# Issuing the 21 transfers that clear the output from GpSimd in one burst instead of from SP among the weights

## The chip, the cores and the metric

The kernel runs on one core of a Trainium2 chip. The metric is the device time of one execution in microseconds. The kernel before takes 942.89 us, the median of three runs (942.83 to 943.75). One more execution was taken with the hardware profiler; all rows below come from that one.

## What is computed

Two branches on the same 2048 x 512 input, mixed by a gate per token. Branch A is a short causal convolution of k, times v, then a long causal convolution per channel (an FFT in the reference) and a product with q. Branch B is a mixture of eight experts with two chosen per token, each a gated MLP with F = 1376 hidden columns.

```python
def _B_ref(x, w_router, w_gate, w_up, w_down):
    logits = jnp.einsum("bsd,de->bse", x, w_router)
    topk_idx = jnp.argsort(logits)[..., -2:]
    gates = _softmax(jnp.take_along_axis(logits, topk_idx, axis=-1), axis=-1)
    ...
    hg = _silu(jnp.einsum("bsd,edf->bsef", x, w_gate))
    hu = jnp.einsum("bsd,edf->bsef", x, w_up)
    y_all = jnp.einsum("bsef,efd->bsed", hg * hu, w_down)
    return jnp.einsum("bse,bsed->bsd", gate_dense, y_all)

x = A_q
g = _sigmoid((x * gate_w).sum(-1, keepdims=True))
a = _A_ref(x, A_k, A_v, A_shift_k, A_ssm_k, A_ssm_D)
b = _B_ref(x, B_w_router, B_w_gate, B_w_up, B_w_down)
return g * a + (1 - g) * b
```

## The kernel before

The eight experts run one after the other (variable `r`), each over eleven tiles of F of 128 columns (`ft`; the last has 96). For a tile, one transfer brings the gate and up weights (`raw`, 512 KB) and one the down weights (`rd`, 256 KB). ScalarE (ACT) rounds them to `gh` and `dh`, VectorE (DVE) computes the remainders `gl` and `dl`, and TensorE (PE) multiplies three times for each product: rows by `gh`, rows by `gl`, remainder of the rows by `gh`. The two products of a half of the rows are `g` and `u`; ACT and DVE make `sg`, `hh` and `hl` of them. After each group of three tiles the down products `yp` go through three PSUM buffers into the sums `ya`, by DVE from the second group on.

The tokens of an expert are fetched by GpSimd (POOL) with indirect transfers (`xg`, five for each expert, L511), turned by TensorE (`xgp`, L520) and split into `xh` and `xl`. The first expert is chosen and gathered ahead of all others, while the routing of the rest is still being worked out (`routing`, `places`, `read_lists`). Results are added into the output rows by indirect transfers from POOL (`add_rows`, L720), so the output, 2688 rows, has to be zero first: `clear` writes 21 blocks of 128 rows from `zt`, a tile of zeros. The first of the adding transfers stands at 168.8 us of the span.

Branch A fills the gaps: `fill` is a list of generators of which `tick` runs a step behind each F tile. `k_stage1` and `x_stage1` are its first stages; `x_stage1` loads the taps `sk` and rows `krow` and `v`, forms `tmp` and `acc` on DVE and splits them into `xs`. Results go through DRAM (`kd`, `xd`, `zd`) between stages. Nine writes left over from the first stages (`rest_k`: `kd` from `ks1`, `ks3`, `ks5`, `ks9`, `ks10` and the load `cr`) are issued by POOL behind the rounding of weight tiles 4, 5 and 6 of the first expert (`behind_rows` adds a wait on the instruction kept in `anchor`; `gh 0 6` is the rounding of tile 6).

SP issues the weights, `krow`, `v` and, in the kernel before, the clearing transfers, in one queue in order; POOL issues in its own. Every transfer of an issuing engine also carries one of eight semaphores in turn, so that it waits for the one that stands eight places earlier to have landed. Up to the end of `order` the instructions stand as written; behind it a scheduler with a model of times orders each engine's instructions, so moving a transfer changes what stands around it. Buffers limit how early SP may load: three for `raw`, two for `rd`; `sk` is also scratch for `places` and is loaded again only behind it.

Of the kernel before, what the change touches and what calls it, by code (L numbers as in the profile page):

```python
# [24 lines left out]
P = 128  # L25
# [12 lines left out]
ROWS = S + TILES * P  # L38
# [15 lines left out]
LG, LR = (2, 5)  # L54
BUB = (1, 1, 3)
XG = 3
Z0, Z1 = (7, 6)
RM = 5
K0, LATE = (4, 3)
SEQ_N = 10  # L60
# [78 lines left out]
def gated_mix(ctx: ExitStack, tc: tile.TileContext, a, out):  # L139
    nc = tc.nc  # L140
    sync, act, dve, pool, pe = nc.sync, nc.scalar, nc.vector, nc.gpsimd, nc.tensor
# [342 lines left out]
    def tick():  # L484
        if fill:
            live.append(fill.pop())
        for g in list(live):
            if next(g, live) is live:
                live.remove(g)
# [3 lines left out]
    def after(engine):  # L493
        return nullcontext() if ordered or engine not in anchor else tc.issue_after(anchor[engine])


    def behind_rows(i, name="act rest"):
        tc.add_manual_dep(i, anchor[name].name, mybir.DependencyInfo(
            mybir.DependencyClass.Sync, mybir.DependencyReason.DATA), reason="behind the gather")

    def tiles(r):
        return (CAPS[r] + P - 1) // P
# [31 lines left out]
    def gather(r):  # L534
        xh = wp.tile([P, KT, CM], F32R, tag="xh", bufs=2, name=f"xh{r}")
        xl = wp.tile([P, KT, CM], F32R, tag="xl", bufs=2, name=f"xl{r}")
        xs[r] = (xh, xl)
        g = [load_rows(r, n) for n in range(XG - 1 if r else tiles(0))]
        for n in range(tiles(r)):
            yield  # L540
            if len(g) < tiles(r):
                g.append(load_rows(r, len(g)))
            turn_rows(r, n, g[n], xh, xl)
# [347 lines left out]
    def places(g):  # L891
        if not g:
            table["hot"] = wp.tile([P, 2, LK, P], F32R, tag="xl", bufs=2, name="hot")
            table["val"] = wp.tile([P, LK, 3, NT], F32R, tag="xh", bufs=2, name="val")
            table["list"] = ps.tile([P, D], F32, tag="y", bufs=3, name="list")[:, :3 * NT]
        hot, val = table["hot"][:, g % 2], table["val"]
        hotc = sk.rearrange("p t d -> p (t d)")[:, g % 2 * 2 * D:][:, :LK * NT].rearrange("p (i c) -> p i c", i=LK)
        part = slice(g * LK, g * LK + LK)
        s3 = [P, LK, NT]
        with after("dve"):  # L900
            dve.tensor_tensor(hot, fl(row)[:, part].unsqueeze(2).to_broadcast([P, LK, P]),
                              io128.unsqueeze(1).to_broadcast([P, LK, P]), op=ALU.is_equal)
            dve.tensor_tensor(hotc, fl(colf)[:, part].unsqueeze(2).to_broadcast(s3),
                              cols.unsqueeze(1).to_broadcast(s3), op=ALU.is_equal)
        for f in range(3):
            dve.tensor_mul(val[:, :, f], hotc, fl(pay[:, f])[:, part].bitcast(F32).unsqueeze(2).to_broadcast(s3))
        for i in range(LK):
            pe.matmul(table["list"], hot[:, i], val[:, i].rearrange("p f c -> p (f c)"),
                      start=(g + i == 0), stop=(g * LK + i == n2 - 1))

    def read_lists():
        pv = table["list"].rearrange("p (f c) -> p f c", f=3)
        dve.tensor_scalar(idf, pv[:, 0], dummy, None, op0=ALU.add)
        dve.tensor_scalar(gidx[:, TILES:], idf[:, TILES:MAIN], float(S - 1), None, op0=ALU.min)
        dve.scalar_tensor_tensor(wsum, idf, float(S), spare, op0=ALU.is_ge, op1=ALU.mult)
        dve.tensor_add(sidx, idf, wsum)
        dve.tensor_copy(wsum, pv[:, 1])
        dve.tensor_add(slot_w, wsum, pv[:, 2])
# [17 lines left out]
    i = dve.tensor_scalar(gidx[:, :TILES], pv0, float(S), float(S - 1), op0=ALU.add, op1=ALU.min)  # L936
# [131 lines left out]

    lv = fp.tile([P, 2 * P], I32, tag="mi", bufs=3, name="lv")[:, :2 * OVER].rearrange("p (o c) -> p o c", c=2)
    def clear(i):  # L1070
        with after("sp"):
            sync.dma_start(out[i * P:(i + 1) * P, :], zt)

    mp = mp_ctx.enter_context(tc.tile_pool(name="moe", bufs=1))
    zt = mp.tile([P, D], F32, tag="yr", bufs=4, name="zt")
# [8 lines left out]
    for r in range(E):  # L1084
        x = expert(r) if r else first
        up, down, finish = x.up, x.down, x.finish
        if r:
            x.begin()
        ends = {g[-1]: i for i, g in enumerate(GROUPS[r])}
        for ft in range(len(FT)):  # L1090
            up(ft)
            for _ in range(min(2, len(tasks))):
                f, *args = tasks.pop(0)
                f(*args)
            if ft in ends:
                tasks.append((down, ends[ft]))
            if r + 1 < E:
                if r == 0:
                    for _ in range(CH.count(ft)):
                        with after("dve rest"), after("act rest"):  # L1100
                            next(rest, None)
                    if 0 <= ft - LG < n2 // LK:
                        places(ft - LG)
                    if ft == LR:
                        read_lists()
                if (r, ft) == (0, LR):
                    dve.tensor_copy(lv[:, :, 0], sidx[:, MAIN:])
                    dve.tensor_copy(lv[:, :, 1].bitcast(F32), slot_w[:, MAIN:])
                    sync.dma_start(lst, lv)
                if ft == (G0 if r == 0 else 4):  # L1110
                    ahead = gather(r + 1)
                if ft >= (G0 if r == 0 else 4):
                    next(ahead, None)
            if r == 0:
                for f in rest_k[LATE * (ft - K0):LATE * (ft - K0 + 1)] if ft >= K0 else ():
                    behind_rows(f.write().ins, f"gh 0 {ft}")
            seen += 1
            if r == 0 and ft >= Z0:
                for i in range(Z1 * (ft - Z0), min(Z1 * (ft - Z0 + 1), ROWS // P)):
                    clear(i)  # L1120
            while done < min(total, int(total * seen / n_up)):
                tick()
                done += 1
        if r not in TM:
            tasks += [(finish, n) for n in range(4)] + [(lambda: None,)] + [(finish, n) for n in range(4, tiles(r))]
# [96 lines left out]
```

## Time and profile before

| | |
|---|---|
| median of three runs | 942.89 us (942.83 to 943.75) |
| profiled execution | 943.57 us, of it 941.3 us span |
| PE busy | 923.5 us, 98% of the span |
| DVE busy | 633.6 us, 67% |
| ACT busy | 509.7 us, 54% |
| POOL busy | 146.6 us, 16% |
| the clearing transfers | 21 of 256 KB, issued by SP from 64.5 to 109.9 us |

Times in the rows are microseconds from the start of the span. A busy share of an engine over the whole span is an average over stages; what matters for a transfer at 64 to 110 us is which engine sets the pace there and at what time the data that this transfer delays is needed. Of an issuing engine the timeline shows when a transfer was issued, not when it landed.

### The profile page before, as it was taken

To read this page: it belongs to the slowest core of one execution; us is meant where nothing else is said; L and a number is where in the kernel's file an instruction comes from. 1 tells how busy PE (TensorE), PEld (TensorE's weight loads), DVE (VectorE), ACT (ScalarE), POOL (GpSimd) and SP (SyncE) were. 2 spreads that over 40 slices of the span, in tenths; PEclk is the share of its full clock that TensorE was granted. 3 is DMA by queue.
4 is the path that set the end of the run, shared out by engine and by line. 5 is a ranking of instruction groups with operands and counts; after the bars stand their busy time and mean duration, and the time that the engine had idled before them with its cause. 6 is when DMAs were issued, how large, how long until landed. Compare 5 with 4: busy or idle time off the path is not lost. (4 is left out here: it accounts for less than half of the span.)

```text
span 941.3 us, 18097 instructions
## 1 busy us (share of the span) xinstructions
PE 923.5 (98%) x6957; PEld 830.0 (88%) x6957; DVE 633.6 (67%) x1131; ACT 509.7 (54%) x883; POOL 146.6 (16%) x137
## 2 busy tenths in 40 slices
PE   8999999999999999999999999999999999999996
PEld 4679999999999999978898889888887989889984
DVE  4796699999996557556767666765777645554541
ACT  4654334755456546478656876668766544234330
POOL 0320210300003020131101211013010310121012
PEclk9999999999999999999999999999999999999999
DMA  9895945754456463456445655456553786787233
GB/s 329 301 349 220 376 153 191 207 193 155 140 202 183 157 205 122 135 135 204 144 136 169 166 181 175 141 167 174 182 172 121 188 276 181 193 200 217 70 54 45
DMA packets 76378, 172.02 MB, mean 183 GB/s; under 512 B 8481, under 2 KB 9377, under 8 KB 76162
## 3 DMA queue, kind: packets, MB, share of 16 engines
q1 hardware_dynamic: 53490, 121.89, 38.4%
q0 software_dynamic: 12464, 29.02, 13.6%
q10 hardware_dynamic: 10336, 19.93, 5.8%
q8 instruction: 56, 0.92, 0.4%
q14 instruction: 32, 0.26, 0.1%
HBM read 127.24 MB, written 43.57 MB: 181 GB/s over the span
## 5 line engine op out<-in xcount | busy, mean ns | idle before, releaser
L200 PE MATMUL u<-xh,gh 128*128 128x256 f32 (+14 forms) x704 | 202.0, 287 | 2.5 <-ACT sg L642 2.5
L200 PE MATMUL g<-xh,gh 128*128 128x256 f32 (+17 forms) x696 | 200.8, 288 | 1.9 <-DVE sg L643 1.9
L202 PE MATMUL u<-xh,gl 128*128 128x256 f32 (+14 forms) x704 | 201.3, 286 | 0.0
L201 PE MATMUL u<-xl,gh 128*128 128x256 f32 (+14 forms) x704 | 201.1, 286 | 0.0
L202 PE MATMUL g<-xh,gl 128*128 128x256 f32 (+17 forms) x696 | 198.8, 286 | 0.0
L201 PE MATMUL g<-xl,gh 128*128 128x256 f32 (+17 forms) x696 | 198.6, 285 | 0.0
L200 PEld LDWEIGHTS g<-xh,gh 128*128 128x128 f32 (+1 forms) x696 | 129.5, 186 | 8.8 <-DVE sg L643 4.5
L200 PEld LDWEIGHTS u<-xh,gh 128*128 128x128 f32 (+1 forms) x704 | 130.9, 186 | 5.9 <-ACT sg L642 3.1
L201 PEld LDWEIGHTS u<-xl,gh 128*128 128x128 f32 (+1 forms) x704 | 130.9, 186 | 4.3 <-issue 4.1
L202 PEld LDWEIGHTS g<-xh,gl 128*128 128x128 f32 (+1 forms) x696 | 129.6, 186 | 4.3 <-issue 4.1
L202 PEld LDWEIGHTS u<-xh,gl 128*128 128x128 f32 (+1 forms) x704 | 131.1, 186 | 0.9 <-issue 0.8
L201 PEld LDWEIGHTS g<-xl,gh 128*128 128x128 f32 (+1 forms) x696 | 129.5, 186 | 2.4 <-issue 0.8
L642 ACT ACTIVATE sg<-g 128x256 f32<-128x256 f32 (+14 forms) x176 | 68.0, 387 | 111.9 <-PE g L202 110.6
L200 PE MATMUL yp<-hh,dh 128*128 128x264 f32 (+13 forms) x440 | 127.1, 290 | 0.0
L202 PE MATMUL yp<-hh,dl 128*128 128x264 f32 (+13 forms) x440 | 126.8, 289 | 0.0
L201 PE MATMUL yp<-hl,dh 128*128 128x264 f32 (+13 forms) x440 | 126.8, 288 | 0.0
L644 ACT ACTIVATE hh<-sg 128x256 fp32r<-128x256 f32 (+14 forms) x176 | 73.1, 418 | 98.6 <-DVE sg L643 98.0
L643 DVE TENSOR_TENSOR sg<-sg,u 128x256 f32<-128x256 f32 (+14 forms) x176 | 74.8, 426 | 72.2 <-PE u L202 70.7
L584 ACT ACTIVATE gh<-raw 128x1024 fp32r<-128x1024 f32 (+1 forms) x88 | 91.4, 1038 | 50.8 <-PE u L201 50.0
L590 DVE TENSOR_TENSOR gl<-raw,gh 128x1024 fp32r<-128x1024 f32 (+1 forms) x88 | 105.3, 1197 | 18.6 <-ACT gh L584 17.8
L645 DVE TENSOR_TENSOR hl<-sg,hh 128x256 fp32r<-128x256 f32 (+14 forms) x176 | 75.0, 429 | 24.8 <-ACT hh L644 24.5
L653 DVE TENSOR_TENSOR dl<-rd,dh 128x512 fp32r<-128x512 f32 (+1 forms) x88 | 59.5, 685 | 39.8 <-ACT dh L651 39.7
(283 smaller groups left out, 1549.6 us busy)
## 6 DMA issues: line engine op xcount, KB each, us to landing
raw<-in_wgu SPq DMA_DIRECT2D x80, 512.0 KB, 4.4
rd<-in_wd SPq DMA_DIRECT2D x80, 256.0 KB, 4.3
kl<-kd SPq DMA_DIRECT2D x16, 512.0 KB, 5.2
xl<-xd SPq DMA_DIRECT2D x32, 256.0 KB, 4.1
zd<-ze ACTq DMA_DIRECT2D x16, 512.0 KB, 3.9
zl<-zd SPq DMA_DIRECT2D x16, 512.0 KB, 5.9
out<-zt SPq DMA_DIRECT2D x21, 256.0 KB, 6.1
krow<-in_kpad SPq DMA_DIRECT2D x19, 256.0 KB, 5.5
```

The costliest lines, as they stand in the source:

```text
L200: pe.matmul(p, wh, hi, start=start, stop=False)
L201: pe.matmul(p, wh, lo, start=False, stop=False)
L202: return pe.matmul(p, wl, hi, start=False, stop=stop)
L584: anchor[f"gh {r} {ft}"] = act.activation(st["gh", ft], raw, AF.Copy).ins
L590: dve.tensor_sub(st["gl", ft][:, c], raw[:, c], st["gh", ft][:, c].bitcast(F32))
L642: act.activation(sg[:fw, :nn], pp[0][:fw, :nn], AF.Silu)
L643: dve.tensor_mul(sg[:fw, :nn], sg[:fw, :nn], pp[1][:fw, :nn])
L644: act.activation(hh[:fw, sl], sg[:fw, :nn], AF.Copy)
L645: dve.tensor_sub(hl[:fw, sl], sg[:fw, :nn], hh[:fw, sl].bitcast(F32))
L653: dve.tensor_sub(dl[:fw], rd[:fw], dh[:fw].bitcast(F32))
```

## The change

`clear` no longer stands in SP's queue. All 21 clearing transfers are issued from POOL when the loop reaches tile 6 of the first expert, each with a wait on `gh 0 6`, behind the nine leftover writes. Before, SP issued six of them behind each of the tiles 7, 8, 9 and the last three behind tile 10 in the order of the source, which the scheduler spread over the queue.

```diff
-Z0, Z1 = (7, 6)
+Z0 = 6
...
     def clear(i):
-        with after("sp"):
-            sync.dma_start(out[i * P:(i + 1) * P, :], zt)
+        return pool.dma_start(out[i * P:(i + 1) * P, :], zt)
...
-            if r == 0 and ft >= Z0:
-                for i in range(Z1 * (ft - Z0), min(Z1 * (ft - Z0 + 1), ROWS // P)):
-                    clear(i)
+            if (r, ft) == (0, Z0):
+                for i in range(ROWS // P):
+                    behind_rows(clear(i).ins, f"gh 0 {Z0}")
```

POOL's queue, the difference from before (-) to after (+), with the gathers `xg` of the second expert (`xg_0` to `xg_4`) behind the last leftover writes:

```order
 L270 DMA kd<-ks10e 256x1x512
 L984 DMA cr<-in_c_r 128x256
+L1071 DMA out<-zt 128x512 x17
 L511 DMA xg_0_1197<-in_q,gidx 128x512
 L511 DMA xg_1_1199<-in_q,gidx 128x512
 L511 DMA xg_2_1380<-in_q,gidx 128x512
-L511 DMA xg_3_1474<-in_q,gidx 128x512
-L511 DMA xg_4_1571<-in_q,gidx 44x512
+L1071 DMA out<-zt 128x512 x4
+L511 DMA xg_3_1495<-in_q,gidx 128x512
+L511 DMA xg_4_1586<-in_q,gidx 44x512
```

Seventeen clearing transfers now stand ahead of the second expert's first gather and four ahead of its fourth.

SP's queue before, from the weights of tile 7 to the rows of the short convolution (`ISA` rows set registers):

```order
L573 DMA raw_8_1495<-in_wgu 128x1024
L623 ISA
L623 DMA rd_8_1565<-in_wd 128x512
L1072 DMA out<-zt 128x512 x6
L573 ISA
L573 DMA raw_9_1586<-in_wgu 128x1024
L1072 DMA out<-zt 128x512 x2
L623 ISA
L623 DMA rd_9_1656<-in_wd 128x512
L1072 DMA out<-zt 128x512 x4
L354 DMA sk<-in_sk 128x2048
L224 DMA krow_1770<-in_kpad 128x512
```

The same place in SP's queue after:

```order
L573 DMA raw_8_1510<-in_wgu 128x1024
L623 ISA
L623 DMA rd_8_1580<-in_wd 128x512
L573 ISA
L573 DMA raw_9_1595<-in_wgu 128x1024
L354 DMA sk<-in_sk 128x2048
L224 DMA krow_1773<-in_kpad 128x512
L623 ISA
L623 DMA rd_9_1665<-in_wd 128x512
L224 DMA krow_1775<-in_kpad 128x512
L224 DMA krow_1777<-in_kpad 128x512
L224 DMA krow_1779<-in_kpad 128x512
```

`sk` and the rows follow directly on the weights of tile 9, with no clearing transfers between.

On DVE the scheduler has answered by moving the short convolution (`tmp`, `acc`) of the first block up, between the additions `ya` of the second group of tiles; this is a piece of the difference:

```order
 L645 TENSOR_TENSOR hl_6_1223<-sg_6_1_1281,hh_6_1222 128x312
+L363 TENSOR_TENSOR tmp_1867<-krow_1777,sk 128x512
 L680 TENSOR_TENSOR ya_0_886<-yp_1_0_256_1303,ya_0_886 128x312
 L680 TENSOR_TENSOR ya_1_909<-yp_1_1_0_1314,ya_1_909 128x256
+L361 TENSOR_TENSOR acc_1866<-krow_1779,sk 128x512
 L680 TENSOR_TENSOR ya_1_909<-yp_1_1_256_1325,ya_1_909 128x312
+L364 TENSOR_TENSOR acc_1866<-acc_1866,tmp_1867 128x512
+L363 TENSOR_TENSOR tmp_1867<-krow_1775,sk 128x512
+L364 TENSOR_TENSOR acc_1866<-acc_1866,tmp_1867 128x512
 L680 TENSOR_TENSOR ya_2_932<-yp_1_2_0_1336,ya_2_932 128x256
```

Ten such operations stand ahead of the last addition of this group (`ya_3`, 312 columns) after, and two before.

On PE the turns `xgp_0` and `xgp_1` of the second expert's rows, of which the first stood within the product `g_7_1` of tile 7 and the second behind the last product of that tile, now stand together within the last product of tile 8, and `xgp_2` behind it:

```order
L200 MATMUL u_8_1_1562<-xh_433,gh_8_1512 128x312
L201 MATMUL u_8_1_1562<-xl_434,gh_8_1512 128x312
L202 MATMUL u_8_1_1562<-xh_433,gl_8_1514 128x312
L200 MATMUL u_8_1_1562<-xh_433,gh_8_1512 128x312
L520 MATMUL xgp_0_1382<-ident,xg_0_1197 128x128 x4
L520 MATMUL xgp_1_1497<-ident,xg_1_1199 128x128 x4
L201 MATMUL u_8_1_1562<-xl_434,gh_8_1512 128x312
```

Both turns now come four matmuls into `u_8_1`, one F tile later than before.

## Rows read from the trace of the kernel before

**Rows 1.** The page, busy time of each engine over the span, and the waits of PE over the whole span (engine, line, what it waited for: us in total, times, longest).

```profile
PE 923.5 (98%) x6957; PEld 830.0 (88%) x6957; DVE 633.6 (67%) x1131; ACT 509.7 (54%) x883; POOL 146.6 (16%) x137
...
PE u L200 <- ACT sg L642: 2.5, 3, 1.6
PE g L200 <- DVE sg L643: 1.9, 2, 1.2
PE xgp L520 <- DMA xg<-in_q,gidx: 1.2, 1, 1.2
```

**Rows 2.** Busy time by stretch: us of the stretch, then busy us (instructions) of PE, PEld, DVE, ACT, POOL, then granted clock, DMA share, GB/s.

```profile
60.00:70.00 10.00, 8.75 (x58) 6.98 (x54) 10.00 (x19) 4.56 (x7) 2.72 (x6) 1.00 0.97 356
...
64.00:320.00 256.00, 256.00 (x1949) 250.84 (x1948) 219.25 (x393) 131.17 (x241) 39.08 (x32) 1.00 0.62 204
320.00:840.00 520.00, 517.48 (x3965) 458.71 (x3965) 329.24 (x539) 314.45 (x510) 79.61 (x74) 1.00 0.55 171
```

**Rows 3.** Timeline of SP's queue (start, us, line, transfer, count).

```profile
64.45 4.98 SPq L1072 DMA_DIRECT2D out<-zt  x6
...
84.11 0.35 SPq L573 DMA_DIRECT2D raw<-in_wgu  x1
85.08 5.40 SPq L1072 DMA_DIRECT2D out<-zt  x6
90.72 1.10 SPq L573 DMA_DIRECT2D raw<-in_wgu  x1
...
98.90 1.62 SPq L354 DMA_DIRECT2D sk<-in_sk  x1
```

**Rows 4.** Timeline of POOL, with the idle time before and its releaser.

```profile
59.73 1.12 POOL L272 DMA_DIRECT2D kd<-ks1e  x2
...
85.81 0.68 POOL L270 DMA_DIRECT2D kd<-ks9e  x1 [15.54 <-ACT gh L584]
86.38 0.83 POOL L270 DMA_DIRECT2D kd<-ks10e  x1
86.94 0.84 POOL L984 DMA_DIRECT2D cr<-in_c_r  x1
94.99 1.04 POOL L511 DMA_INDIRECT xg<-in_q,gidx  x1 [7.21 <-PE g L202]
...
122.02 3.36 POOL L511 DMA_INDIRECT xg<-in_q,gidx  x1 [5.30 <-PE xgp L520]
```

**Rows 5.** Time from issue to landing: transfers issued from 84 to 96 us, one after the other (KB each, us), and the gathers issued from 60 to 130 us.

```profile
kd<-ks9e POOLq DMA_DIRECT2D x1, 512.0 KB, 6.9
kd<-ks10e POOLq DMA_DIRECT2D x1, 512.0 KB, 8.2
cr<-in_c_r POOLq DMA_DIRECT2D x1, 128.0 KB, 8.7
...
DMA to landing us min/median/max: 5.3/6.6/6.9
```

**Rows 6.** DMA queues, packets, MB and share of 16 engines: POOL's (q0) and SP's (q1) from 36 to 50 us, when both had work throughout. Then the same stretch and three later ones by engine, in the columns of Rows 2.

```profile
q0 software_dynamic: 720, 2.62, 47.8%
q1 hardware_dynamic: 914, 2.45, 46.6%
...
36.00:50.00 14.00, 14.00 (x98) 12.11 (x97) 10.46 (x38) 7.83 (x15) 3.62 (x5) 1.00 1.02 394
...
84.00:96.00 12.00, 12.00 (x98) 12.00 (x98) 8.97 (x22) 4.96 (x9) 2.99 (x4) 1.00 0.93 341
96.00:104.00 8.00, 8.00 (x61) 8.00 (x61) 4.04 (x8) 2.26 (x4) 1.97 (x3) 1.00 1.04 392
...
112.00:120.00 8.00, 8.00 (x60) 7.07 (x59) 8.00 (x15) 5.05 (x9) 2.02 (x2) 1.00 0.97 316
```

**Rows 7.** Timeline of PE: the first two turns of the second expert's rows and what follows each, a down product of the second group that takes a PSUM buffer again, and the first matmul of the second half of tile 8 (`g_8_1`).

```profile
105.03 0.29 PE L200 MATMUL yp<-hh,dh 128*128 128x256 f32 x1
...
112.31 0.60 PE L520 MATMUL xgp<-ident,xg 128*128 128x128 f32 x4
112.66 0.39 PE L200 MATMUL g<-xh,gh 128*128 128x312 f32 x1
...
114.90 0.60 PE L520 MATMUL xgp<-ident,xg 128*128 128x128 f32 x4
115.43 1.13 PE L293 MATMUL ks0p<-kr,c 64*128 64x512 f32 x4
...
119.41 0.31 PE L200 MATMUL g<-xh,gh 128*128 128x312 f32 x1
```

**Rows 8.** Timeline of DVE with idle time before, and its busy time from 101.5 to 110.5 us (us, busy us, instructions, clock, DMA share, GB/s).

```profile
87.49 1.22 DVE L590 TENSOR_TENSOR gl<-raw,gh 128x1024 fp32r<-128x1024 f32 x1
...
101.93 0.91 DVE L680 TENSOR_TENSOR ya<-yp,ya 128x312 f32<-128x312 f32 x2
...
110.57 0.69 DVE L363 TENSOR_TENSOR tmp<-krow,sk 128x512 f32<-128x512 f32 x1 [1.51 <-DMA krow<-in_kpad]
111.18 0.68 DVE L653 TENSOR_TENSOR dl<-rd,dh 128x512 fp32r<-128x512 f32 x1
111.78 0.69 DVE L361 TENSOR_TENSOR acc<-krow,sk 128x512 f32<-128x512 f32 x1
...
101.50:110.50 9.00, 3.14 (x8) 1.00 1.04 403
```

## The prediction

> **What bounds the kernel now.** I read the waits of PE and its busy time by stretch first, then the two queues that issue the clearing transfers, and last the places where PE or DVE first needs something that those transfers can delay.
>
> PE is busy for 98% of the span, and the stretch that matters is tighter than that: from 64 us, just before the first clearing transfer is issued, to 320 us PE is busy for all of its 256.00 us, and no wait of PE is listed there [rows 1, 2]. The reader should keep this apart from what SP does in the same stretch. SP issues its first six clearing transfers in 4.98 us and six more in 5.40 us, 0.8 to 0.9 us each where one weight transfer takes 0.35 us, and the weights of tile 9 follow at 90.72 us, although the last reader of their buffer (`gl` of tile 6, from 87.49 for 1.22 us) ended at 88.7 us [rows 3, 8]. So the clearing transfers do hold up SP by 2 us or so. But no one waits for what SP brings later: `sk`, issued at 98.90 us, makes DVE wait 1.51 us once (the row names `krow`, which follows it), and even that doesn't reach PE [rows 3, 8]. SP's queue is not what sets the end.
>
> **Removed from SP: 0 us.** The 21 issues cost SP 15 to 19 us of its own time (21 x 0.7 to 0.9 us), none of it on PE. After the change, `raw` of tile 9 can go at 88.7 instead of 90.72 us, `sk` right behind it at some 89 instead of 98.90 us. PE already has every weight in time, so an earlier weight gives it nothing; a gain would need a wait of PE between 64 and 320 us, and there is none. Behind 320 us PE has 2.52 us without work in the next 520 us [rows 2], in places that both kernels reach with the same instruction order on PE (the two orders of PE come together again at about a third of the queue, some 310 us in). I take no gain, and bound it at 2.5 us.
>
> **Added to POOL: the burst.** 21 more plain transfers at the spacing of the `kd` writes, 0.56 us each (two in 1.12 us), are 11.8 us of issuing [rows 4]. POOL stood idle for 7.21 us from the end of `cr` to the gather at 94.99 us, so some of that lies in an idle time. The wait on `gh 0 6` adds nothing: `ks9`, ahead in the queue, waits for the same instruction and goes at 85.81 us [rows 4]. Each of POOL's transfers also waits for the one eight places earlier to land. The first five clearing transfers go out at once from about 87.5 us, and the rest at the pace of the landings.
>
> What is queued behind: the second expert's gathers `xg_0` to `xg_2`, before issued from 94.99 us on. They now land when POOL's share of the DMA engines has moved the 1.18 MB of `ks9`, `ks10` and `cr`, then 17 x 0.262 = 4.46 MB of zeros, then 0.262 MB for each gather: 5.90 MB until `xg_0` is there. From 84 us SP's queue moves in that time, by its order, `raw` of tiles 8, 9, 10 and the next expert's 0 (0.524 MB, the third 0.393), four `rd` (three of 0.262, the last 0.197), `sk` (1.05), five `krow` and two `v` (0.262 each) and a small list: 5.9 MB. Together 11.8 MB.
>
> When is that done? Three prices. By the total, at the 392 GB/s of 96 to 104 us, in 30.1 us from 84.5 us: 114.6 us. At the 341 GB/s of 84 to 96 us: 119.1 us. With POOL's queue at the rate at which it moved 1.18 MB from 85.81 until `cr` landed (86.94 + 8.7 = 95.6 us), 120 GB/s, the remaining 4.72 MB take 39 us: 135 us [rows 4 to 6]. The last is too high: in 39 us SP's queue would have to move more than the 5.9 MB it has. When both queues had work throughout, from 36 to 50 us, they took nearly equal parts, 2.62 and 2.45 MB at 394 GB/s together [rows 6]; an equal part, 195 GB/s, from 85.8 us for 5.90 MB gives 116 us. I take 116 us, and 114.6 to 119 us as the likely span.
>
> When does PE need it? PE's work is the same up to 112.31 us, where `xgp_0` stood. In the new order `xgp_0` and `xgp_1` come four matmuls into the last product of tile 8. `g_8_1` started at 119.41 us; without the two turns ahead (112.66 - 112.31 = 0.35 and 115.43 - 114.90 = 0.53 us) it starts at 118.5 us; 16 matmuls of 0.144 us (119.41 to 121.14 us were twelve) bring PE to `xgp_0` at 120.8 us, and eight more and the turns to `xgp_2` at 122.7 us [rows 7]. `xg_0` at 116 us is 4.8 us early; `xg_1` and `xg_2` follow by 0.7 to 1.3 us each and are early too. So the delay of the gathers, 10 us or more, is covered by work of tiles 7 and 8 that the scheduler has put ahead of the turns, and this margin of about 5 us is the thinnest cover in the change. The four clearing transfers ahead of `xg_3` go out while `xgp_0` is still to come, and `xg_3` needs that turn to free its buffer anyway: 0 us. The adding transfers at 168.8 us wait for all 21 to land; the last is there by some 125 us: 0 us.
>
> **Moved on DVE.** Ten operations of the short convolution now stand ahead of the last addition of the second group, eight more than before. At 0.60 us from start to start (111.18 to 111.78 us) that is 4.9 us, and DVE stood idle for 9.00 - 3.14 = 5.9 us of that very stretch, waiting for PE's down products [rows 8]. They fit, but only if the rows are there: the first `tmp` stands at about 101.9 us, and needs `sk` and the third `krow`. From 88.7 us SP's queue has `raw` of tile 9 (0.524), `sk` (1.05), three `krow` and an `rd` (1.05 MB) until then, 2.62 MB at an equal part of 195 GB/s in 13.4 us: 102 us; with a landing delay of 1 to 2 us perhaps 103 to 104 us. DVE may then wait 0 to 2 us. PE first feels it at the PSUM buffer that the second addition frees (101.93 us) and `yp` takes again at 105.03 us [rows 7, 8], so 3.1 us are free. Cost 0 us, with 0 to 3 us kept for the range.
>
> **Sum.** 0 - 0 + 0 + 0. The profiled execution would stay at 943.57 us, 0.68 us (0.07%) above the median of 942.89; I forecast the median: 942.9 us.
>
> **Rivals.**
>
> *The gathers come late (slower).* POOL's queue gets less than an equal part, `xg_0` lands after 120.8 us, and PE stands at `xgp_0`, with all products behind it. It decides at a mean rate of 4.72 / (120.8 - 95.6) = 187 GB/s for POOL's queue from 95.6 us on. At the mean of the two rates that I have, 157 GB/s, it lands at 125.7 us: 4.9 us lost, 947.8 us; at 120 GB/s 14 us, 957 us. For it: the 120 GB/s were measured at this very place, and the first expert's gather made PE wait for 1.2 us too [rows 1]. Against it: SP's queue runs dry at buffers that are not free yet, and what it doesn't move POOL's can. Chance 0.14, half of it under 3 us.
>
> *DVE waits for the rows.* `sk` and `krow` come 4 us or more after 101.9 us, DVE holds the `ya` additions and PE's PSUM buffers: lateness minus 3.1 us, say 1 to 4 us, 944 to 947 us. Chance 0.05.
>
> *Writing the transfers on POOL is slow beside DVE.* One gather took 3.36 us where others took 1.04 [rows 4]. If each of 17 clearing transfers took that long, `xg_0` would be issued at 87.5 + 57 = 144.6 us, land 5.3 us later [rows 5] and hold PE for 29 us: 972 us. Against it: `kd<-ks1e` went at 0.56 us each in a stretch in which DVE was busy for 10.00 of 10 us [rows 2, 4]. The Trainium skill (SBUF — State Buffer, section "SBUF: two separate sides") has the rule behind this rival: a VectorE operation that uses both ports keeps GpSimd from writing the descriptors of its transfers, and issuing from SP or ACT avoids it. By that rule the change would be a clear loss; the trace agrees at most for the one gather, and no run here shows it for plain writes. Chance 0.02.
>
> *Faster.* DVE gets the short convolution done earlier and is freer from 110 us on, and later waits of PE go: at most the 2.52 us of rows 2, 940.4 us. PE's time from 64 to 320 us has nothing to give. Chance 0.05.
>
> **How the numbers follow.** No change 0.74, late gathers 0.14, late rows 0.05, slow writing 0.02, faster 0.05. 0.2%, about what a measurement of this kernel can tell from no change, is 1.9 us. Of the late cases about 0.04 is under that and counts as the same, and of the faster 0.01: faster 0.04, same 0.79, slower 0.17. The range reaches down to 941.8 us (a gain of 1 us and the scatter of the runs) and up to 946.5 us, which takes in the shorter waits of the two late cases and leaves out about 0.09 above and 0.04 below.
>
> **What would show it.** Right: POOL issues clearing transfers from 87 to 88 us, five at once and then paced by landings; `xg_0` lands from 114 to 119 us; the PE waits list no DMA at `xgp` of the second expert; PE is again busy for 256 of 256 us from 64 to 320 us; `sk` is issued at about 89 us and DVE is no longer idle between the additions from 102 to 110 us. Wrong: a wait of PE for `xg` at about 121 us (the first rival, its length being the loss), PE waiting for DVE's `ya` from 105 to 112 us (the second), clearing transfers of 2 us or more on POOL (the third), or a difference that arises behind 320 us, where I expect none.

## The result: slower by 0.9%

| | before | after |
|---|---|---|
| median | 942.85 us (22 runs, 941.07 to 951.31) | 950.68 us (22 runs, 948.28 to 961.48) |
| ratio | | 1.0089, 95% interval 1.0066 to 1.0112 |
| profiled execution | 943.57 us | 951.6 us, of it 949.8 us span |

Ratios, here and below, leave disturbed runs out, so they can differ a little from the ratio of the medians. The time is outside the range of the prediction (941.8 to 946.5 us), on the side that was given 0.17.

I read the waits of PE first, from 64 to 320 us. Before, none was listed there [rows 1]; now there are three of size (engine, line, what it waited for: us in total, times, longest).

```profile
PE yp L200 <- DVE tmp L363: 3.4, 1, 3.4
PE g L200 <- DVE sg L643: 1.2, 2, 0.9
PE u L200 <- ACT sg L642: 1.0, 1, 1.0
```

The busy time by stretch, in the columns of [rows 2], gives the size and the place.

```profile
64.00:320.00 256.00, 250.25 (x1893) 243.88 (x1892) 214.41 (x387) 124.59 (x233) 46.73 (x50) 1.00 0.60 201
320.00:840.00 520.00, 517.36 (x3979) 459.38 (x3978) 329.34 (x540) 316.05 (x514) 79.03 (x74) 1.00 0.55 170
...
100.00:140.00 40.00, 35.36 (x261) 33.48 (x260) 31.06 (x56) 13.96 (x27) 10.88 (x14) 1.00 0.80 287
```

PE now stands for 5.75 of the 256 us in which it never stood [rows 2], and 4.64 of them lie between 100 and 140 us. Behind 320 us nothing has changed (517.36 of 520 us; before, 2.52 us without work). The timeline of DVE shows what holds PE; it answers to [rows 8].

```profile
100.91 0.48 DVE L645 TENSOR_TENSOR hl<-sg,hh 128x312 fp32r<-128x312 f32 x1
107.36 0.69 DVE L363 TENSOR_TENSOR tmp<-krow,sk 128x512 f32<-128x512 f32 x1 [5.98 <-DMA krow<-in_kpad]
107.97 0.81 DVE L680 TENSOR_TENSOR ya<-yp,ya 128x312 f32<-128x312 f32 x2
...
114.90 0.69 DVE L361 TENSOR_TENSOR acc<-krow,sk 128x512 f32<-128x512 f32 x1 [2.36 <-DMA out<-zt]
```

```profile
104.88 0.28 PE L202 MATMUL u<-xh,gl 128*128 128x256 f32 x1
108.50 0.39 PE L200 MATMUL yp<-hh,dh 128*128 128x256 f32 x1 [3.35 <-DVE tmp L363]
```

The second fence is PE's timeline. DVE stands for 5.98 us at the first `tmp` until the third `krow` is there; the two additions `ya` behind it in DVE's queue start only at 107.97 us, and they free the PSUM buffers. PE has other products (`g` and `u`) until 105.15 us, then stands for 3.35 us at the next `yp` and goes on at 108.50. The rest of the 4.64 us are shorter stops; the longest, 0.86 us at 118.50 us, is for a `sg` that DVE reaches late, behind the `acc` in the last line of the first fence (it reads a `krow`, though the row names a clearing transfer).

SP issued the rows early enough, and POOL wrote its transfers quickly. First SP's queue, then POOL's; they answer to [rows 3, 4].

```profile
88.12 0.33 SPq L573 DMA_DIRECT2D raw<-in_wgu  x1
88.49 1.43 SPq L354 DMA_DIRECT2D sk<-in_sk  x1
90.04 1.32 SPq L224 DMA_DIRECT2D krow<-in_kpad  x1
91.62 1.34 SPq L623 DMA_DIRECT2D rd<-in_wd  x1
93.05 3.05 SPq L224 DMA_DIRECT2D krow<-in_kpad  x3
```

```profile
86.86 2.97 POOL L1071 DMA_DIRECT2D out<-zt  x5
90.40 0.54 POOL L1071 DMA_DIRECT2D out<-zt  x1 [0.57 <-DMA kd<-ks9e]
...
103.09 0.54 POOL L1071 DMA_DIRECT2D out<-zt  x1 [0.52 <-DMA out<-zt]
104.51 1.04 POOL L511 DMA_INDIRECT xg<-in_q,gidx  x1 [0.88 <-DMA out<-zt]
```

What was slow is the transport. The DMA queues from 88.5 us, where `sk` is issued, to 107.3 us, where the third `krow` is there (packets, MB, share of 16 engines; q0 is POOL's, q1 SP's):

```profile
q0 software_dynamic: 1455, 4.49, 62.7%
q1 hardware_dynamic: 1018, 2.92, 40.0%
```

In 18.8 us POOL's queue moved 4.49 MB, 239 GB/s, and SP's 2.92 MB, 155 GB/s. An equal part of these 395 GB/s would have brought SP's 2.92 MB in 14.8 us, by 103.3 us: within the 103 to 104 us that the prediction had reckoned.

### The profile page after: what moved, and what is told of

It reads as the page before. It is cut to its first block, busy times and chain, and to the rows that moved or that the text cites. A ratio compares the mean times of both kernels' runs of the same rounds, so it can differ in the third digit from the quotient of the medians.

```text
span 949.8 us, 18093 instructions
## 1 busy us (share of the span) xinstructions
PE 925.5 (97%) x6957; PEld 830.4 (87%) x6957; DVE 632.8 (67%) x1131; ACT 506.9 (53%) x883; POOL 157.5 (17%) x158
## 2 busy tenths in 40 slices
DMA packets 75034, 172.02 MB, mean 181 GB/s; under 512 B 8481, under 2 KB 9377, under 8 KB 74818
## 5 line engine op out<-in xcount | busy, mean ns | idle before, releaser
L200 PEld LDWEIGHTS yp<-hh,dh 128*128 128x128 f32 (+1 forms) x440 | 82.8, 188 | 7.1 <-DVE tmp L363 3.6
```

The costliest lines, as they stand in the source:

```text
L200: pe.matmul(p, wh, hi, start=start, stop=False)
```

## The experiments

My theory after this (A): POOL's burst takes more than half of the DMA engines; the rows that DVE has been given ahead of `ya` come late; DVE holds PE. Rivals: (C) the new order on DVE costs by itself; (D) the clearing transfers cost by themselves, through POOL's writing or what they move, wherever they stand. All kernels are edits of the changed one.

| kernel | median us (before beside it) | ratio, 95% interval |
|---|---|---|
| e1_hold | 945.55 (942.09) | 1.0030, 0.9994 to 1.0066 |
| e2_early | 951.83 (942.09) | 1.0120, 1.0077 to 1.0163 |
| e3_none | 943.25 (942.09) | 1.0011, 1.0000 to 1.0023 |
| e4_small | 949.39 (942.09) | 1.0076, 1.0043 to 1.0109 |
| e5_half | 956.37 (941.97) | 1.0128, 1.0088 to 1.0169 |
| e6_late | 954.09 (941.97) | 1.0126, 1.0078 to 1.0175 |
| e7_spread | 950.69 (941.97) | 1.0077, 1.0040 to 1.0113 |
| e8_four | 948.29 (942.44) | 1.0066, 1.0036 to 1.0095 |
| e9_drip | 952.17 (942.44) | 1.0087, 1.0054 to 1.0119 |
| e10_strided | 950.08 (942.28) | 1.0064, 1.0033 to 1.0094 |
| e11_cols | 951.19 (942.28) | 1.0092, 1.0050 to 1.0135 |
| e12_late_hold | 946.67 (942.24) | 1.0034, 1.0008 to 1.0060 |

### The burst without the order, and the order without the burst

e1_hold keeps the burst and makes the taps on DVE wait for the last addition of the second group.

```diff
-        dve.tensor_mul(acc, krow(pl), sk[:, 0])
+        with after("ya 1"):
+            dve.tensor_mul(acc, krow(pl), sk[:, 0])
...
+            if (r, g, dc) == (0, 1, KT - 1):
+                anchor["ya 1"] = i.ins
```

> The changed kernel with the short convolution on DVE held behind the last addition ya of the second group; the queues of SP and POOL are the same, transfer for transfer. Theory A (the burst makes sk and krow late, DVE stands at tmp ahead of the additions, PE's PSUM buffers stay full): the rows land as late as before, at 106 to 107 us, but PE doesn't wait for DVE at 105 to 109 us; at most 1 to 2 us of waits are left around 112 to 118 us; 943 to 945 us. Theory B (the loss comes from the burst itself in the DMA engines, by late weights or late gathers, and the place of the convolution is a side show): still 949 to 952 us. Theory C (PE's and ACT's changed order from 100 to 310 us costs by itself): still some 948 us or more.

Measured 945.55 us, half a microsecond above what theory A had expected. DVE still waits for a row, but behind the additions, and PE's waits from 64 to 320 us (second fence) shrink to 1.2 us.

```profile
109.79 0.47 DVE L681 TENSOR_TENSOR ya<-yp,ya 128x312 f32<-128x312 f32 x1
...
114.97 0.69 DVE L362 TENSOR_TENSOR acc<-krow,sk 128x512 f32<-128x512 f32 x1 [3.51 <-DMA krow<-in_kpad]
```

```profile
PE u L200 <- ACT sg L643: 0.8, 1, 0.8
PE u L200 <- DVE sg L644: 0.4, 1, 0.4
```

e3_none keeps the short convolution among the additions and issues one clearing transfer; the other 20 blocks are not cleared.

```diff
-                for i in range(ROWS // P):
+                for i in range(1):
```

> The changed kernel with one clearing transfer in place of 21: 20 blocks of the output are not cleared, so that work is left out. The convolution stands as early on DVE as in the changed kernel, or earlier. Theory A: the third krow lands at 96 to 98 us, no wait of DVE, 941 to 944 us; that the convolution stands among the additions costs nothing when its rows are there. Theory C: 948 us or more, since the order has moved as much.

Measured 943.25 us. `tmp` stands among the `ya` here too, but its row is there: the wait is 0.33 us, where it was 5.98. (This profiled execution is some 6 us late throughout, for a reason given in the last section, so its waits compare with the others and its times do not.)

```profile
106.19 0.69 DVE L363 TENSOR_TENSOR tmp<-krow,sk 128x512 f32<-128x512 f32 x1 [0.33 <-DMA krow<-in_kpad]
```

So neither the burst alone (1.0030) nor the order alone (1.0011) costs what both together do (1.0089). Rival C falls for the stretch of the burst, and so does D as the main cause. Near 300 us e3_none's order on ACT is not that of the changed kernel (below, under the amount), so there it says nothing about C.

### The burst at other places

e2_early puts the whole burst one tile earlier, e6_late four tiles later.

```diff
-Z0 = 6
+Z0 = 5
...
-Z0 = 6
+Z0 = 10
```

> All 21 clearing transfers from POOL one tile earlier, behind the rounding of tile 5 (about 69 us), where the DMA engines stood idle from 75 to 83 us. Theory A: the burst is over by 86 us, the third krow lands before 101 us, DVE doesn't wait for it, 942 to 944 us, as before the change. Theory B: a burst costs wherever it stands, 946 us or more, with waits for weights of tile 6 or 7. Theory C: the order on DVE is nearly that of the changed kernel, so 948 us or more.

Measured 951.83 us: not better. DVE has its rows for `tmp` now, but the burst met another load. From 83 to 88 us SP's queue moved 0.26 of 1.45 MB, ACT stood for `rd`, and PE waited 2.2 us at 90 us for the `sg` behind it on ACT; a second wait of 3.0 us ends at 299 us (below, under the amount). The first fence shows the queues, the second ACT's timeline.

```profile
q0 software_dynamic: 358, 1.20, 86.4%
q1 hardware_dynamic: 116, 0.26, 13.8%
```

```profile
89.37 0.63 ACT L651 ACTIVATE dh<-rd 128x512 fp32r<-128x512 f32 x1 [5.36 <-DMA rd<-in_wd]
```

e5_half leaves ten transfers in the burst and puts eleven behind `gh 0 10`; e7_spread and e9_drip cut it up.

```diff
+# e5_half
+Z0 = {6: (0, 10), 10: (10, 21)}
+# e7_spread
+Z0 = {6: (0, 6), 7: (6, 11), 8: (11, 16), 9: (16, 21)}
+# e9_drip
+Z0 = {5: (0, 3), 6: (3, 6), 7: (6, 9), 8: (9, 13), 9: (13, 17), 10: (17, 21)}
...
-            if (r, ft) == (0, Z0):
-                for i in range(ROWS // P):
-                    behind_rows(clear(i).ins, f"gh 0 {Z0}")
+            if r == 0 and ft in Z0:
+                for i in range(*Z0[ft]):
+                    behind_rows(clear(i).ins, f"gh 0 {ft}")
```

> Ten of the 21 clearing transfers stay in the burst behind gh 0 6, and eleven wait for gh 0 10 (about 124 us). The first ten operations of the short convolution stand on DVE exactly as in the changed kernel, so only the amount of data that meets the rows is halved. If the loss is the lateness of krow behind the burst: eleven transfers are 2.88 MB, 11.5 us at the 250 GB/s that POOL's queue took; the third krow lands near 103 us in place of 107, DVE waits under 2.5 us for it and PE not at all for ya: 942 to 945 us. If the order on DVE alone, or the writing of transfers by POOL at whatever time, costs the time: 948 to 951 us as the changed kernel.

> All 21 clearing transfers wait for gh 0 10 (about 124 us), behind the rows of the short convolution and behind the second expert's gathers. If the loss is the meeting of the burst with loads that are needed at once: from 124 us SP brings raw and rd of the second expert; PE's stretch from 64 to 120 us is free of the ya wait, 942 to 945 us, or again 945 to 950 us with a wait of ACT or DVE for raw, rd or for the adding transfers at 168 us, if the burst meets loads as urgent as the first. If the burst costs wherever it stands, by its writing on POOL: 948 to 951 us, with no wait for a load behind it.

> 6, 5, 5 and 5 clearing transfers wait for gh 0 6, gh 0 7, gh 0 8 and gh 0 9. The scheduler puts eleven ahead of the second expert's gathers and ten behind; those behind gh 0 7 can't go before about 96 us. If the loss is the share that SP's queue loses to POOL's while sk and krow are on their way (88 to 102 us): the six go until about 93 us, the third krow lands near 103 us, no wait of PE for ya, 942 to 945.5 us. If only the total of data up to 107 us counts: eleven to sixteen transfers compete all the same, a DVE wait of 3 to 5 us, 945 to 948 us. If POOL's writing costs: 948 to 951 us.

> All 21 transfers, 3, 3, 3, 4, 4 and 4 behind gh 0 5 to gh 0 10; in POOL's order six stand between cr and the gathers, three of these only from about 96 us. Theory (SP's loads are late for as long as POOL's queue has work, and PE has about 3 us of cover at each place): 3 transfers and the writes are 2.0 MB from 86 us, empty at 94 us; then 0.79 MB and the gathers, 1.6 MB, to about 102 us: the third krow at 104 to 106 us, PE waits 0 to 2 us for ya, and a little at later places, 943 to 947 us; better than the three forms with longer bursts (950.7 to 956.4 us). Rival (POOL's writing beside DVE or the transfers as such cost, not the bunching): 948 to 952 us as those.

All four stayed at 950.7 to 956.4 us, so I had mis-sized this. In e5_half the row came as late with ten transfers as with 21 (first fence, DVE): leftover writes, zeros and gathers still gave POOL's queue 1.79 MB against SP's 1.08 from 97 to 104 us (second fence), and my 942 to 945 us had counted the transfers that were gone, not the moment at which the queue runs dry. In e6_late the burst met the rows of a later block, and the same picture came back (third fence, DVE; fourth, PE).

```profile
107.07 0.69 DVE L363 TENSOR_TENSOR tmp<-krow,sk 128x512 f32<-128x512 f32 x1 [6.85 <-DMA krow<-in_kpad]
```

```profile
q0 software_dynamic: 544, 1.79, 62.9%
q1 hardware_dynamic: 538, 1.08, 39.7%
```

```profile
137.00 0.69 DVE L361 TENSOR_TENSOR acc<-krow,sk 128x512 f32<-128x512 f32 x1 [4.17 <-DMA krow<-in_kpad]
...
138.60 0.47 DVE L680 TENSOR_TENSOR ya<-yp,ya 128x312 f32<-128x312 f32 x1
```

```profile
139.13 0.58 PE L200 MATMUL yp<-hh,dh 128*128 128x256 f32 x1 [3.87 <-DVE ya L680]
```

e7_spread had the row at 107.21 us after 6.78 us of waiting, e9_drip PE waits of 2.2, 1.2 and 1.2 us. These runs alone would also suit rival D, which says that the burst costs wherever it stands; e12_late_hold decides that.

### The amount

e8_four issues four clearing transfers; the other 17 blocks are not cleared.

```diff
-                for i in range(ROWS // P):
+                for i in range(4):
```

> Only the first four of the 21 blocks are cleared, in the burst at the old place; 17 blocks are not cleared. DVE's order around the second ya is that of the changed kernel but for one acc that stands two places earlier. With ten transfers in the burst the third krow landed at 106.9 us, with 21 at 107.2: POOL's queue was busy at 250 to 265 GB/s until 104 us in both, SP's had 150. Here POOL's queue has 1.18 MB of leftover writes, 1.05 MB of zeros and 0.79 MB of gathers, 3.0 MB; at 250 GB/s from 86 us it is empty at about 98 us, and SP's queue has the DMA engines alone from there. Theory (the share while POOL's queue has work): third krow by 103 to 104 us, DVE waits under 3 us, PE under 0.5 us for ya, 942.5 to 945 us. Rival (the order on DVE, or any clearing transfer ahead of the gathers, costs whatever its amount): 947 to 951 us.

The row came at 101.95 us, before the 103 to 104 expected, and the `ya` wait is gone. The time, 948.29 us, is above what I expected. The profiled execution (946.44 us) has one long wait left, 2.1 us at 295 us, where ACT has stood for an adding transfer and the rounding `gh`, which feeds PE, stands behind it (first fence DVE, second ACT, third PE; the fourth is ACT at the same place in e3_none).

```profile
101.95 0.69 DVE L363 TENSOR_TENSOR tmp<-krow,sk 128x512 f32<-128x512 f32 x1 [1.74 <-DMA krow<-in_kpad]
```

```profile
293.15 0.68 ACT L716 ACTIVATE yr<-yt,slot_w 44x512 f32<-44x512 f32 x1 [4.42 <-DMA out<-yr,sidx]
...
294.25 1.04 ACT L584 ACTIVATE gh<-raw 128x1024 fp32r<-128x1024 f32 x1
```

```profile
295.59 0.39 PE L200 MATMUL g<-xh,gh 128*128 128x272 f32 x1 [2.12 <-DVE sg L643]
```

```profile
297.21 1.06 ACT L584 ACTIVATE gh<-raw 128x1024 fp32r<-128x1024 f32 x1 [0.70 <-PE u L201]
300.33 0.68 ACT L716 ACTIVATE yr<-yt,slot_w 44x512 f32<-44x512 f32 x1 [2.06 <-DMA out<-yr,sidx]
```

This is a second term. The changed kernel has it with 1.0 us (`u` for `sg`, behind an `yr` that waited 4.11 us), and so have e2_early (3.0), e5_half (2.9), e6_late (2.2), e7_spread (1.9), e9_drip (1.2), e4_small (0.9) and e10_strided (0.5). The kernel before, e1_hold, e3_none, e11_cols and e12_late_hold have no wait of PE there. The traces show what parts the two groups: in all nine with the wait ACT has a `gh` right behind this `yr`, or behind it and one `xs`; in all five without it that rounding went ahead of the `yr`, which stands for at most 2.9 us there. That is the pattern of `tmp` and `ya` again, on another engine; but no run changes this order by itself, so it is not shown as a cause.

The rest of e8_four's 5.9 us (948.29 - 942.44) is open. In its profiled execution PE stands for 2.84 of the 256 us, these 2.1 among them; of its longer executions (up to 954.88 us) there is no profile. So e8_four does not show that the time comes back when the rows come early: it is still at 1.0066.

### The size of the rows

e4_small, e10_strided and e11_cols move the same zeros in other shapes.

```diff
-        return pool.dma_start(out[i * P:(i + 1) * P, :], zt)
+# e4_small, 32 transfers
+        return pool.dma_start(flat_out[:, i * ZW:(i + 1) * ZW], zt[:, :ZW])
+# e10_strided, 21 transfers
+        return pool.dma_start(out.rearrange("(p a) d -> p a d", p=P)[:, i, :], zt)
+# e11_cols, 42 transfers
+        b, c = i // 2, i % 2 * 256
+        return pool.dma_start(out[b * P:(b + 1) * P, c:c + 256], zt[:, :256])
```

> The burst behind the rounding of tile 6 again, but as 32 transfers of 128 x 336 elements, rows of 1344 bytes in place of 2048; the bytes are the same. In the trace of the changed kernel POOL's packets are 4096 bytes, two rows each, and SP's krow packets 2048, and both queues get through the same number of packets. If the engines take packets in turn, and if rows of 1344 bytes go one to a packet, SP's queue gets more than half of the bytes in place of 40%, the third krow lands at 100 to 102 us in place of 106 to 107, DVE waits under 2 us and the time is 943 to 946 us. If queues share by bytes or by backlog instead, the rows land at 105 to 107 us and the time stays at 949 us or more.

> Same bytes, same 21 transfers, same place and order; a transfer writes every 21st row of the output instead of 128 rows in one piece, so that two rows can't be joined in DRAM. In the changed kernel POOL's clearing transfers went as packets of 4096 bytes (two rows) and SP's rows as 2048, in about equal numbers: 250 to 265 against 150 GB/s. If the packets become 2048 bytes and the queues take turns packet by packet: about 195 GB/s each, the third krow (2.6 MB of SP's queue) by 104 to 105 us, PE waits 0 to 1.5 us for ya, 943 to 946.5 us. If the packets stay at 4096, or the share doesn't hang on their size: 250 to 150 GB/s again, third krow at 107 us, 948 to 951 us.

> Same bytes in 42 transfers of 128 rows of 1024 bytes; 17 of them, 2.23 MB, stand ahead of the second expert's gathers and 25 behind. If they go as packets of 1024 bytes, as the load cr of 128 x 256 did, and the queues take turns packet by packet: POOL's queue 130 to 160 GB/s, SP's 250 and more, third krow by 103 us, no PE wait for ya, 942.5 to 946 us, with the gathers late as the new risk. If they are joined to 4096 bytes (or the share doesn't hang on the size): SP's queue at 150 GB/s until about 104 us as with ten transfers, third krow at 106 to 107 us, a PE wait of 3 to 5 us, 948 to 956 us.

All three stay slow. The queues from 98 to 100 us, in the changed kernel, e10_strided, e4_small and e11_cols, one fence each:

```profile
q0 software_dynamic: 152, 0.50, 61.5%
q1 hardware_dynamic: 144, 0.31, 39.0%
```

```profile
q0 software_dynamic: 162, 0.53, 65.0%
q1 hardware_dynamic: 162, 0.29, 38.1%
```

```profile
q0 software_dynamic: 134, 0.46, 56.4%
q1 hardware_dynamic: 200, 0.36, 47.2%
```

```profile
q1 hardware_dynamic: 226, 0.41, 53.8%
q0 software_dynamic: 148, 0.41, 51.2%
```

With rows of 2048 bytes POOL's queue has 1.6 to 1.8 times SP's bytes, joined or strided; with 1344 bytes 1.3 times; with 1024 bytes as much as SP's. The smaller the rows, the less DVE waited for the `krow`: 5.98 us (changed kernel) and 6.48 us (e10_strided) with 2048 bytes, 4.32 us with 1344 and 3.48 us with 1024. The first condition of e10_strided did not come about: its execution has 75034 packets, as the changed kernel's has, so two rows still went together. I had expected turns packet by packet; in e4_small and e11_cols POOL's 0.67 and 0.65 packets for each of SP's don't fit that. With the rows the transfers shrank too (256, 168 and 128 KB), and so did what POOL can have under way, since each waits for the one eight places earlier; these runs don't part the two. By what rule the queues share is left open.

e11_cols also shows the price of getting out of the way only once: its wait at `yp` is down to 0.9 us, its burst lasts to 123 us and meets the next row, and PE loses the time there (DVE, then PE).

```profile
130.83 0.69 DVE L361 TENSOR_TENSOR acc<-krow,sk 128x512 f32<-128x512 f32 x1 [3.76 <-DMA krow<-in_kpad]
```

```profile
131.97 0.63 PE L200 MATMUL g<-xh,gh 128*128 128x312 f32 x1 [3.47 <-DVE sg L643]
```

### The late burst with no tap ahead of PE's work

e12_late_hold is e6_late with the edit of e1_hold, on the third group's last addition.

```diff
+        with after("ya 2"):
+            dve.tensor_mul(acc, krow(pl), sk[:, 0])
...
+            if (r, g, dc) == (0, 2, KT - 1):
+                anchor["ya 2"] = i.ins
```

> The late burst (all 21 behind gh 0 10, about 122 to 145 us), and on DVE all taps of the short convolution wait for the last addition of the third group (about 149 us), so that in the stretch of the burst no tap with its krow stands ahead of a ya or sg. If the loss of the late burst (954.1 us; acc waited up to 4.2 us for krow at 124.9 and 137.0 us, and PE 3.9 us for ya and 2.2 us for sg behind it) comes from taps that the order has put ahead of PE's operations while the rows are late: the ya wait goes, 942 to 946.5 us, with whatever rd or raw in the burst still cost ACT (dh waited 5.1 us once). If the burst costs in itself, by what it takes from the weights: 948 to 954 us with waits of ACT for rd or raw in place of those.

Measured 946.67 us, 0.2 us above the first range, against 954.09 for the same burst without the hold. First PE's busy time around the burst in e6_late, where POOL issues it from 122.6 to 138.3 us. The profiled execution of e12_late_hold runs some 8 us later, and there the burst is issued from 130.7 to 145.5 us (second fence, with PE's longest wait from 64 to 320 us).

```profile
100.00:140.00 40.00, 34.48 (x257) 33.06 (x256) 31.04 (x58) 14.21 (x27) 14.61 (x24) 0.97 0.70 257
```

```profile
130.00:160.00 30.00, 30.00 (x227) 28.84 (x226) 19.42 (x37) 10.53 (x21) 16.84 (x24) 1.00 0.86 312
...
PE xs2p L279 <- DVE xs L218: 2.1, 1, 2.1
```

This execution, 955.2 us, was the longest of the twelve and already behind before 62 us, so its total isn't used. With all 21 transfers issued and landing PE works 30.00 of 30 us. The wait for `xs` comes at 195 us; I put it down to the hold, which makes DVE finish the convolution later, but no run shows that. The second term of e6_late, 2.2 us at 303 us, is gone here too, so not all of the 7.4 us between the two runs need come from the taps. What the runs show: it is not the burst as such (D); it is what the order has put on DVE ahead of PE's operations while the burst makes the rows late. No version beats the kernel before: the best ones with the burst end 0.3% above it, e1_hold with an interval that just takes in no change.

## Why the prediction was wrong

*What bounds the kernel, and SP: right.* Taking the transfers off SP's queue gains nothing: e3_none, with 20 of them gone altogether, is at 1.0011.

*The burst on POOL: right in its cost, with some luck.* The single clearing transfers took 0.54 to 0.59 us each, five went out at once and the rest at the pace of the landings, and no PE wait names a gather. But the 116 us for `xg_0` used the same equal part as the step that failed below. POOL's queue got more: it had moved 5.95 MB, all that goes up to `xg_0`, between 85.2 and 112 us, and PE came to the turn at 125.33 us in place of 120.8. The error made the cover wider. The rival *gathers come late* did not happen.

Nor did *slow writing*. The last four clearing transfers took 0.54 to 0.59 us each between 108.09 and 111.34 us, while DVE was busy for 2.93 of 3.25 us, no longer than the 0.54 us of those from 101.10 to 103.63 us, while DVE was busy for 0.28 of 2.53 us. By the rule of the Trainium skill (SBUF — State Buffer, section "SBUF: two separate sides") that was quoted there, a VectorE operation that uses both ports keeps GpSimd from writing descriptors. For these plain writes the trace doesn't show it; it doesn't speak against the rule either, since the rows don't say which of DVE's operations use both ports. The prediction's "clear loss" by that rule took for granted that they do.

*Moved on DVE: here it failed.* The step was "2.62 MB at an equal part of 195 GB/s". The equal part came from 36 to 50 us [rows 6]. At the place in question SP's queue had 155 GB/s and POOL's 239; the third `krow` came at 107.3 us in place of 103 to 104, and DVE waited 5.98 us in place of 0 to 2. A smaller part of the error is the amount: SP's queue brought 2.92 MB, not 2.62, from 88.5 us until then. I had a row that showed unequal parts at this very place, and used it only for POOL's queue: 120 GB/s. There POOL's queue had the smaller part (1.18 MB against SP's 2.41 from 85.8 to 95.6 us), so it didn't say which queue would lose; as a bound for SP's part it would have given 21.8 us for the 2.62 MB, 110.5 us. The sum's "Cost 0 us" for this measured 4.64 us of PE's time.

*The cover.* "3.1 us are free" counts from the start of the addition, 101.93 us, to PE's `yp`, 105.03 us [rows 7, 8]. PE came to that `yp` at 105.15 us, so the end of the count held. Its start did not: in the new order the late `tmp` stands ahead of the addition, and PE went on only 1.14 us after `tmp` had started, 0.61 us for `tmp` and 0.53 us until the addition had freed the buffer. That leaves about 2 us.

*The rival that happened* was "DVE waits for the rows", with the right mechanism and direction, given 0.05; its sign, PE standing between 105 and 112 us, is the 3.35 us above. Its formula, lateness minus 3.1 us, gives 5.4 - 3.1 = 2.3 us for the lateness measured, 945 us; PE stood for 3.35 us at this place, 1 us more by the cover, and for 1.3 us at later places that the formula leaves out. Of the span's 8.5 us (949.8 - 941.3) 5.75 are PE's idle time from 64 to 320 us. Of these 5.75, about 1 us is the second term, at 301 us. PE's own busy time over the span is 2.0 us longer (925.5 against 923.5 us for the same 6957 instructions), which I have not traced further.

*The sign behind 320 us: right*, there is no difference there.

## What to carry to other kernels

A transfer that is moved to another queue still takes from the same DMA engines, and in a burst it may take more than half: price the loads of the other queue at the lowest part that the trace shows anywhere, not at an equal one. Then look which operation stands first behind such a load on an engine that feeds the bottleneck; an order made for early loads turns a late one into a stall, and holding those operations back was worth more here than moving or cutting the burst. Count the cover to the moment at which the buffer is free, with the time of the late operation and of the one behind it.

## What the runs showed of the hardware

The granted clock fell after some of PE's stalls. In e11_cols PE was busy for 3.53 of 7 us, and in the next 7 us the mean granted clock was 0.64, between the two levels of 1.2 and 2.4 GHz.

```profile
126.00:133.00 7.00, 3.53 (x25) 3.27 (x24) 3.24 (x6) 2.00 (x4) 1.61 (x2) 0.87 0.78 296
133.00:140.00 7.00, 7.00 (x37) 7.00 (x35) 6.66 (x14) 2.15 (x4) 0.00 (x0) 0.64 0.36 112
```

The changed kernel's profile shows 1.00 from 100 to 140 us in spite of its stall, so a stall did not always bring this on. Apart from any change, e3_none's profiled execution (949.7 us, 6.5 above its median) ran at the lower level of 1.2 GHz from 10 to 25 us; times near 950 us among the runs of the kernel before may have the same cause, but no profile of it shows one. The clock alone need not be it: e9_drip's and e12_late_hold's profiled executions had got through as few matmuls in this stretch (98 and 97, against 129 in the kernel before), and their rows give a granted clock of 1.00. That is left open.

```profile
10.00:25.00 15.00, 14.77 (x96) 8.64 (x97) 5.39 (x20) 3.79 (x19) 0.00 (x0) 0.50 0.84 311
```
